# One normalisation and one transpose per slot, and the last 64 keys on GpSimd's queue, in a fused attention and MoE kernel

## The chip, the cores and the metric

The kernel runs on one core of a Trainium2 chip. A core has five engines that run side by side, each through its own instruction queue in order: TensorE (matmuls; PE, and PEld for its weight loads), VectorE (DVE), ScalarE (ACT), GpSimd (POOL) and SyncE (SP), which here only issues DMAs. DMAs are issued from a queue of an engine, run on 16 shared DMA engines, and tell by a semaphore when they have landed. The metric is the time of the device for one execution in microseconds (us). Before the change the median of 8 runs is 525.76 us (521.06 to 527.22).

## The reference

Thresholded attention, then a two-layer feed-forward block with a hard-swish gate. The shapes are 8 batches, 8 heads, 576 positions, head size 64; the block has 4608 rows, width 512 and inner width 2048.

```python
scores = scale * np.matmul(q, k.transpose(0, 1, 3, 2))
thresh = np.max(scores, axis=-1, keepdims=True) - tau
scores = np.where(scores >= thresh, scores, -1000000000.0)
attn = np.exp(scores - np.max(scores, axis=-1, keepdims=True))
attn = attn / (np.sum(attn, axis=-1, keepdims=True) + 1e-09)
x = np.matmul(attn, v)          # then heads side by side: [4608, 512]
h = x @ w_in
g = h * np.clip(h + 3.0, 0.0, 6.0) / 6.0
out = g @ w_out
```

## The kernel before

**Slots.** Four heads of one batch are a quad, two of them a pair; there are 16 quads. A quad is worked through in 9 slots: slots 0 to 3 take the first pair, 128 query rows each, slots 4 to 7 the second pair, and slot 8 the last 64 query rows of both pairs. That makes 144 slots, numbered n = 0 to 143. One loop over n writes all instructions of all engines in a hand-made order, and each engine runs its own in that order. A slot has two score tiles of 128 by 576, one per head.

**One slot's weights.** TensorE writes the scores into PSUM (`scores`, L287). VectorE copies them to the tile s in SBUF and takes the row maximum (`sm_max`, L302); GpSimd makes a bias from the maximum (L305). ScalarE masks by threshold (`sm_mask`, L309) and takes the exponential with the row sum (`sm_exp`, L314). VectorE inverts the sum (`sm_recip`, L317), GpSimd multiplies by it and writes bf16 into the tile pn (`sm_norm`, two instructions, L322). At the end of `sm_norm` SP issues a DMA that transposes pn into pT (or pR for slot 8), L330; in the first 21 slots TensorE does some of these transposes instead (`on_chip`). There are 4 buffers of pn and 4 of s. The product with the values (`multiply`, L346 and L349) comes some slots later, in columns of 256 queries.

**The loop from slot 22 on (N1 = 22).** In slot n VectorE takes the maxima for slot n + 1; ScalarE does the exponential of slot n and the mask of slot n + 1. Even slots start with the relu of the feed-forward block on ScalarE, odd ones do it on VectorE. In both, VectorE then does the gate (`mm1_gate`, L404), which reads the first matmul's PSUM bank (`mm1`, L381 or L376). After it in an even slot TensorE does two parts of the second matmul (`mm2_part`, L415), and then the next slot's `mm1` into the same bank. The product with the values and the scores of two later slots come in odd slots. Odd slots also finish the weights of two slots: the list `ready` holds the even slot and the odd one, whose reciprocals are taken in the odd slot (the even slot's after the maxima, L541; the odd slot's own near the end, L594), and both are normalised and transposed at its end (L613). The loop's end then issues waiting output DMAs (`flush`, L436), loads of q and k on SP (L620), and loads of values or of the block's weights on GpSimd (L622 to L625).

**Loads.** For quads 4 to 15, q and k come in blocks of 32 columns which VectorE transposes (`blocks_q`, L94, and `blocks_k`, L99, four DMAs each per pair of heads). The last 64 keys of each head go to the tile kr by two DMAs of 64 partitions (`rest`, L126), and TensorE transposes them (L257). `loads` is a list of jobs; a slot starts the next one, from slot 37 on only in even slots. The jobs of such a quad are: keys of the first pair, queries of the first pair, the last 64 keys with the keys of the second pair (`both`), queries of the second pair. Values come by GpSimd's queue (L143 and L146).

**After the loop.** The last products with the values are interleaved with the remaining feed-forward work: `av_main` for the last pair's first columns, the items left in `todo1`, eight items of the last batch, then the last columns and `av_rest`, which reads the transposed weights of slot 143.

Of the kernel before, what the change touches and what calls it, by code (L numbers as in the profile page):

```python
# [20 lines left out]
def kernel(  # L21
# [60 lines left out]
    def load_quad(quad):  # L82
        b, g = divmod(quad, 2)
        nat[quad] = (nat_pool.tile([P, 1152], F32, tag="nq", name="nq"),
                     nat_pool.tile([P, 4, 4, D], F32, tag="km", name="km"),
                     nat_pool.tile([P, 2 * D], F32, tag="kr", name="kr"))
        nq, km, kr = nat[quad]

        def main(dst, src, h, order, by=nc.sync):
            by.dma_start(out=dst[:, :, h, :], in_=src[b, 4 * g + h, 0:512, :].rearrange(order, t=4))  # L90

        def blocks_q(n, a, j):
            c = 32 * (2 * a + j)
            nc.sync.dma_start(out=nq[c:c + 32, n * S:(n + 1) * S].rearrange("p (k d) -> p k d", d=32),  # L94
                              in_=q[b, 4 * g + 2 * n + a, :, 32 * j:32 * j + 32].rearrange("(k r) d -> r k d", r=32))

        def blocks_k(n, a, j):
            c = 32 * (2 * a + j)
            nc.sync.dma_start(  # L99
                out=km[c:c + 32].rearrange("p t h d -> p (t h d)")[:, n * 512:(n + 1) * 512].rearrange(  # L100
                    "p (t m d) -> p t m d", t=4, d=32),
                in_=k[b, 4 * g + 2 * n + a, 0:512, 32 * j:32 * j + 32].rearrange("(m r t) d -> r t m d", r=32, t=4))

        def load_k(n):
            if b < NB:
                for a in range(2):
                    main(km, k, 2 * n + a, "(p t) d -> p t d")
            else:
                for a in range(2):
                    for j in range(2):  # L110
                        blocks_k(n, a, j)

        def load_q(n):
            if b < NB:
                for a in range(2):
                    main(nq[:, 0:1024].rearrange("p (t h d) -> p t h d", h=4, t=4), q, 2 * n + a, "(t p) d -> p t d",
                         by=nc.scalar if quad == n == 0 else nc.sync)
            else:
                for a in range(2):
                    for j in range(2):  # L120
                        blocks_q(n, a, j)

        def rest():
            for dst, src in ((kr[:], k), (nq[:, 1024:1152], q))[0:2 if b < NB else 1]:
                for n in range(2):
                    nc.sync.dma_start(out=dst[64 * n:64 * n + 64, :].rearrange("p (h d) -> p h d", h=2),  # L126
                                      in_=src[b, 4 * g + 2 * n:4 * g + 2 * n + 2, 512:S, :].rearrange("h p d -> p h d"))

        def both():
            rest()  # L130
            load_k(1)

        if b < NB:
            loads.extend((lambda: load_k(0), lambda: load_q(0), rest, lambda: load_k(1), lambda: load_q(1)))
        else:
            loads.extend((lambda: load_k(0), lambda: load_q(0), both, lambda: load_q(1)))

    def load_v(b):
        vm = v_pool.tile([P, H, 4 * D], BF16, tag="vm", name="vm")
# [176 lines left out]
    def sm_recip(sl):  # L316
        nc.vector.reciprocal(out=sl.rinv[:], in_=sl.rsum[:])  # L317

    def sm_norm(sl):
        sl.pn = pn = pn_pool.tile([P, 2, S], BF16, tag="pn", name="pn")  # L320
        for i in range(2):
            nc.gpsimd.tensor_scalar(out=pn[:, i, :], in0=sl.s[:, i, :], scalar1=sl.rinv[:, i:i + 1], scalar2=1.0,  # L322
                                    op0=Alu.mult, op1=Alu.mult)
        if sl.slot < 8:
            pair, t = 2 * sl.quad + sl.slot // 4, sl.slot % 4
            sl.dst = pts[pair][:, :, t * P:(t + 1) * P]
        else:
            sl.dst = ptr[sl.quad][:, :, :]
        if not sl.on_chip:
            nc.sync.dma_start_transpose(out=sl.dst, in_=pn[:].rearrange("p a b -> p (a b)"))  # L330
# [181 lines left out]
        return copies  # L512

    prev = None
    ready = []
    last_keys = []
    part = 0
    waiting = []
    for n, sl in enumerate(queue):
        quad, slot = sl.quad, sl.slot  # L520
        b, g = divmod(quad, 2)
        now = n
        if slot in (0, 4):
            pts[2 * quad + slot // 4] = pt_pool.tile([P, 9, 512], BF16, tag="pT", name="pT")
        if slot == 8:
            ptr[quad] = ptr_pool.tile([P, 9, P], BF16, tag="pR", name="pR")
        for ahead in {0: (1, 2), 9: (3,), 16: (4,)}.get(n, (quad + 2,) if quad > 2 and slot == (2 if quad == 3 else 0) else ()):
            if ahead < NQUAD:
                load_quad(ahead)
        if slot == 0 and g == 1 and b + 1 < B:  # L530
            load_v(b + 1)
        for copy in last_keys:
            copy()
        last_keys = []
        if 0 < n <= N1:
            for i in range(2):
                sm_exp(prev, i)
        if n + 1 < len(queue):
            sm_max(queue[n + 1])
        even = n >= N1 and n % 2 == 0  # L540
        for old in ready:  # L541
            sm_recip(old)
        for copy in waiting:
            copy()
        waiting = []

        if todo1:
            item, then = todo1.pop(0)
            h = mm1(item, OB if n > N1 and n % 2 and not pieces else HB)
            todo2.extend(then)  # L550
        else:
            item = None
        if n >= N1:
            for copy in multiply(n):
                copy()
        if item:
            mm1_gate(item, h, mm1_relu(h, on_act=even))
        copies = pe_transpose(queue[n - 2]) if n > 1 and queue[n - 2].on_chip else None
        if prev is not None and n < N1:
            sm_recip(prev)  # L560
        if copies:
            copies()
        pieces = 2 if n % 2 == 0 and todo2 else 0
        for _ in range(pieces):
            bb, mt, part = todo2.pop(0)
            mm2_part(bb, mt, part)
        if n <= N1:
            for i in range(2):
                sm_mask(sl, i)
        if n == N1:  # L570
            sm_recip(prev)
        if n >= N1:
            for i in range(2):
                sm_exp(sl, i)
            if n + 1 < len(queue):
                for i in range(2):
                    sm_mask(queue[n + 1], i)
        if n < N1:
            for copy in multiply(n):
                copy()  # L580
        if part == 3:
            waiting.append(lambda tile=(bb, mt): late.extend(mm2_out(*tile, on_act=False)))
            part = 0
        evict = []
        for job, of in turns.get(n, ()):
            if job == "k":
                (last_keys if even else evict).append(transpose_k(of))
            elif job == "q":
                if of // 2 not in qkT:
                    alloc_qk(of // 2)  # L590
                (waiting if even else evict).append(transpose_q(of))
            else:
                (last_keys if even else evict).append(transpose_rest(of, of_k=of > 0))
        if n >= N1 and not even:  # L594
            sm_recip(sl)
        for out_of_psum in evict:
            if out_of_psum:
                out_of_psum()
        if n == 0:
            warm_up(8)  # L600
        if n <= N1:
            scores(n + 2)
        elif n % 2:
            for m in (n + 3, n + 2):
                if m < len(queue):
                    scores(m)
        if n < 8:
            warm_up(6)
        if 0 < n <= N1:
            sm_norm(prev)  # L610
        if n >= N1:
            ready.append(sl)
        if n > N1 and not even:  # L613
            for old in ready:
                sm_norm(old)
            ready = []
        flush()
        if n == 0:
            start(loads, 2)
        elif n not in (4, 12, 15, 18, 21) and not 23 < n < 30 and (n < 37 or n % 2 == 0):  # L620
            start(loads, 1)
        if n < 4 or 15 < n < 20 or n > 33:  # L622
            start(vcasts, 1 if n < N1 or n % 2 else 0)
        else:
            start(casts, 2 if n in (5, 8, 11, 14) or 21 < n < 28 else 1)  # L625
        prev = sl
# [31 lines left out]
    av_main(2 * last + 1, 0, 256)()  # L658
    for item in todo1:
        rest1(*item, on_act=False)  # L660
    head, tail = moe_of(B - 1)
    for item in head:
        rest1(*item)
# [41 lines left out]
```

## Time and profile before

| | before |
|---|---|
| median of 8 runs | 525.76 us (521.06 to 527.22) |
| profiled execution, its time | 521.54 us |
| profiled execution, its span | 519.8 us |
| granted TensorE clock | 1.00 |
| TensorE busy | 506.1 us, 97% |
| VectorE, ScalarE, GpSimd busy | 441.7, 453.0, 285.4 us |
| DMAs issued by SP for q, k and kr blocks (L94, L99, L126) | 96, 96 and 40 |
| transposes issued by SP for pn | 131 |

The span runs from the first to the last instruction; the execution's own time has 1.7 us more around it. Times in the rows are us from the span's start. A row of a timeline gives start, length, engine, line, operation, output and input tiles, and in brackets the engine's idle time before it and what ended it. A row of the chain gives start, length and what the end of the program was waiting for then. "x4" at a row means that four instructions in succession are merged into it. SPq and POOLq are what the sequencers of SP and GpSimd do: they issue DMAs and wait. TensorE's busy share is high even where it is slowed, so lengths of whole slot pairs are compared where it matters.

### The profile page before, as it was taken

What the parts mean: (1) busy time and instruction counts of PE and PEld (TensorE: products, weight loads), DVE (VectorE), ACT (ScalarE), POOL (GpSimd) and SP (SyncE); (2) the same over time, 40 slices, a digit from 0 to 9 for tenths busy, and PEclk for the clock granted to TensorE, in tenths of its full rate; (3) what the DMA queues carried; (4) which work ended last, traced back from release to release, by engine and by line L of the source; (5) the groups of instructions that cost most, each with busy time, mean ns of one, the idle gap of its engine ahead of it and who ended that gap; (6) DMA issues with size and microseconds to landing.
All of it is one profiled execution on the core that took longest, in us unless ns stands there. A gap on an engine that the chain in (4) does not pass through costs nothing.

```text
span 519.8 us, 12073 instructions
## 1 busy us (share of the span) xinstructions
PE 506.1 (97%) x4145; PEld 321.3 (62%) x4145; DVE 441.7 (85%) x1124; ACT 453.0 (87%) x980; POOL 285.4 (55%) x514
## 2 busy tenths in 40 slices
PE   8999999999999999999999999999999999999997
PEld 6765556666665666666655666666655666668463
DVE  3788888999999999999999999999999999888151
ACT  4999979999999999999999999999999999995060
POOL 1788868855666665666556655666556655552000
PEclk9999999999999999999999999999999999999999
DMA  5899999979999898999999997999999996553222
GB/s 131 129 167 159 154 153 142 197 127 170 163 170 187 161 177 144 188 164 169 160 167 181 170 190 133 179 163 174 167 159 182 167 177 122 121 112 82 81 62 61
DMA packets 316780, 78.75 MB, mean 152 GB/s; under 512 B 299696, under 2 KB 312240, under 8 KB 316720
## 3 DMA queue, kind: packets, MB, share of 16 engines
q1 hardware_dynamic: 297920, 68.69, 75.1%
q0 software_dynamic: 17600, 8.92, 14.6%
q8 instruction: 32, 0.52, 0.4%
q10 hardware_dynamic: 1200, 0.39, 0.3%
q14 instruction: 28, 0.23, 0.2%
HBM read 36.70 MB, written 9.44 MB: 89 GB/s over the span
## 4 chain that ended last, share of the span: by engine, by line
PE 68%; ACT 8%; POOL 3%; DVE 3%; issue 2%; DMA 2%; SPq 0%; POOLq 0%; DVEq 0%
PE ps L415 20%; PE ps L287 20%; PE ps L381 18%; PE ps L346 6%; ACT s L309 4%; POOL pn L322 3%; ACT s L314 2%; PE ps L376 2%; ACT r L389 1%; PE ps L349 1%; DMA pT<-pn 1%; DVE s L302 1%; DVE g L404 1%; DMA g<-go 1%; ACT kT L222 0%
## 5 line engine op out<-in xcount | busy, mean ns | idle before, releaser
L322 POOL TENSOR_SCALAR pn<-s,rinv 128x576 bf16<-128x576 f32 x288 | 211.1, 745 | 82.5 <-issue 53.7
L302 DVE TENSOR_SCALAR_CACHE_REDUCE s<-ps 128x576 f32<-128x576 f32 x288 | 205.5, 751 | 15.2 <-PE ps L287 9.4
L309 ACT ACTIVATE s<-s,bias 128x576 f32<-128x576 f32 x288 | 205.9, 762 | 7.8 <-POOL bias L305 7.2
L314 ACT ACTIVATE s<-s 128x576 f32<-128x576 f32 x288 | 192.4, 670 | 0.3
L287 PE MATMUL ps<-kT,qT 64*128 64x384 f32 (+7 forms) x1280 | 174.0, 419 | 4.1 <-DVE s L302 3.1
L287 PEld LDWEIGHTS ps<-kT,qT 64*128 64x128 f32 (+1 forms) x1280 | 103.7, 175 | 58.6 <-issue 15.6
L415 PE MATMUL ps<-w_out_sb,g 128*128 128x512 bf16 x576 | 134.0, 379 | 0.0
L381 PE MATMUL ps<-xT,w_in_sb 128*128 128x256 bf16 x1024 | 130.8, 273 | 1.0 <-DVE g L404 0.7
L381 PEld LDWEIGHTS <-w_in_sb 128*128 128x128 bf16 x1024 | 95.4, 98 | 41.1 <-issue 21.7
L404 DVE SCALAR_TENSOR_TENSOR g<-r,ps 128x512 bf16<-128x512 f32 x128 | 87.5, 687 | 11.4 <-ACT r L389 7.4
L415 PEld LDWEIGHTS <-g 128*128 128x128 bf16 x576 | 56.2, 98 | 56.7
L305 POOL TENSOR_SCALAR bias<-m 128x2 f32<-128x2 f32 x144 | 27.2, 189 | 102.8 <-DVE rinv L317 84.2
L389 ACT ACTIVATE r<-ps,three 128x512 f32<-128x512 f32 x81 | 55.2, 687 | 26.8 <-PE ps L381 19.5
L314 ACT ACTIVATION_READ_ACCUMULATOR s<-s 128x1 f32 x288 | 54.3, 189 | 0.0
L391 DVE TENSOR_SCALAR r<-ps 128x512 f32<-128x512 f32 x63 | 42.9, 681 | 0.0
L346 PE MATMUL ps<-pT,vm 128*64 128x256 bf16 (+1 forms) x480 | 39.1, 285 | 0.0
L346 PEld LDWEIGHTS <-vm 128*64 128x64 bf16 x736 | 27.2, 110 | 16.0 <-issue 14.3
L357 DVE CAST xT<-ps 128x256 bf16<-128x256 f32 (+1 forms) x60 | 26.3, 438 | 12.6 <-PE ps L349 12.6
L423 DVE TENSOR_SCALAR osb<-ps 128x512 f32<-128x512 f32 x31 | 20.8, 673 | 12.6 <-PE ps L415 12.6
L302 DVE DVE_READ_ACCUMULATOR s<-ps 128x1 f32 x288 | 23.9, 83 | 0.0
L317 DVE RECIPROCAL rinv<-rsum 128x2 f32<-128x2 f32 x144 | 21.3, 148 | 2.6 <-ACT s L314 2.6
L143 POOL DMA_DIRECT2D vm<-in_v_dram x28 | 21.2, 758 | 0.1
(56 smaller groups left out, 244.1 us busy)
## 6 DMA issues: line engine op xcount, KB each, us to landing
out_dram<-osb SPq DMA_DIRECT2D x31, 256.0 KB, 2.6
nq<-in_q_dram SPq DMA_DIRECT2D x96, 72.0 KB, 3.4
km<-in_k_dram SPq DMA_DIRECT2D x96, 64.0 KB, 3.2
vm<-in_v_dram POOLq DMA_DIRECT2D x24, 128.0 KB, 4.1
km<-in_k_dram SPq DMA_DIRECT2D x16, 128.0 KB, 3.5
w_in_sb<-in_moe_w_in_dram POOLq DMA_DIRECT2D x16, 128.0 KB, 3.8
w_out_sb<-in_moe_w_out_dram POOLq DMA_DIRECT2D x16, 128.0 KB, 3.9
pT<-pn SPq DMA_TRANSPOSE x117, 3.7
```

What stands on the lines that cost most here:

```text
L287: nc.tensor.matmul(ps_flat[rows, c0:c0 + w], qT_of(pair)[a * 64:(a + 1) * 64, q0:q0 + rows.stop - rows.start], kT_of(pair)[a * 64:(a + 1) ...
L302: nc.vector.tensor_scalar(out=sl.s[:, i, :], in0=ps_flat[:, c0:c0 + S], scalar1=1.0, scalar2=None, op0=Alu.mult, op1=Alu.max, accum_out=sl ...
L305: nc.gpsimd.tensor_scalar(out=sl.bias[:], in0=sl.m[:], scalar1=-scale, scalar2=tau, op0=Alu.mult, op1=Alu.add)
L309: nc.scalar.activation(out=s, in_=s, func=Act.Prelu, bias=sl.bias[:, i:i + 1], scale=scale, alpha=REJECT)
L314: nc.scalar.activation(out=s, in_=s, func=Act.Exp, accum_out=sl.rsum[:, i:i + 1])
L322: nc.gpsimd.tensor_scalar(out=pn[:, i, :], in0=sl.s[:, i, :], scalar1=sl.rinv[:, i:i + 1], scalar2=1.0, op0=Alu.mult, op1=Alu.mult)
L346: nc.tensor.matmul(pb[a * 64:(a + 1) * 64, :], vm[:, 2 * hp + a, c * D:(c + 1) * D], pT[:, 5 * a + c, cols], start=(c == 0), stop=False)
L381: nc.tensor.matmul(ps[:, hb, n * 256:(n + 1) * 256], w_in_sb[:, ki, (ni + n) * P:(ni + n + 1) * P], xT[b][:, ki, c0:c0 + 256], start=(ki = ...
L389: nc.scalar.activation(out=r, in_=hps, func=Act.Relu, bias=three[:])
L391: nc.vector.tensor_scalar(out=r, in0=hps, scalar1=3.0, scalar2=0.0, op0=Alu.add, op1=Alu.max)
L404: nc.vector.scalar_tensor_tensor(out=out, in0=r, scalar=6.0, in1=hps, op0=Alu.min, op1=Alu.mult)
L415: nc.tensor.matmul(o_ps[0], gbuf[:, ni, mt * P:(mt + 1) * P], w_out_sb[:, ni, :], start=(ni == 0), stop=(ni == NI - 1))
```

## The change

From slot 22 on, each slot normalises the slot before it. An even slot's weights are thus treated where they were before, at the end of the following odd slot; an odd slot's reciprocal moves to the following even slot, after that slot's maxima, and its normalisation and transpose move to that slot's end. The list `ready` is gone. The last slot's are placed after the loop, behind the items of `todo1`. For quads 4 to 15 the two loads of the last 64 keys go out from GpSimd's queue instead of SP's, and the load jobs have another order: queries, keys, queries of the second pair, then the last 64 keys with the second pair's keys.

```diff
-                    nc.sync.dma_start(out=dst[64 * n:64 * n + 64, :].rearrange("p (h d) -> p h d", h=2),
+                    (nc.sync if b < NB else nc.gpsimd).dma_start(out=dst[64 * n:64 * n + 64, :].rearrange("p (h d) -> p h d", h=2),
                                       in_=src[b, 4 * g + 2 * n:4 * g + 2 * n + 2, 512:S, :].rearrange("h p d -> p h d"))
...
-            loads.extend((lambda: load_k(0), lambda: load_q(0), both, lambda: load_q(1)))
+            loads.extend((lambda: load_q(0), lambda: load_k(0), lambda: load_q(1), both))
...
-    ready = []
...
-        for old in ready:
-            sm_recip(old)
+        if n > N1:
+            sm_recip(prev)
...
-        if n >= N1 and not even:
-            sm_recip(sl)
...
-        if 0 < n <= N1:
+        if n > 0:
             sm_norm(prev)
-        if n >= N1:
-            ready.append(sl)
-        if n > N1 and not even:
-            for old in ready:
-                sm_norm(old)
-            ready = []
...
     for item in todo1:
         rest1(*item, on_act=False)
+    sm_recip(prev)
+    sm_norm(prev)
     head, tail = moe_of(B - 1)
```

## The prediction

> **What bounds the kernel now.** I read the busy shares first, then the chain that ended last in an undisturbed stretch, then the places where that chain leaves TensorE, then the queue that they lead to.
>
> ```profile
> PE 506.1 (97%) x4145; PEld 321.3 (62%) x4145; DVE 441.7 (85%) x1124; ACT 453.0 (87%) x980; POOL 285.4 (55%) x514
> PE 68%; ACT 8%; POOL 3%; DVE 3%; issue 2%; DMA 2%; SPq 0%; POOLq 0%; DVEq 0%
> ```
>
> Four engines are above 84%, so a share alone settles nothing. The chain between 254 and 282 us does (start, length, work):
>
> ```profile
> 261.09 2.14 PE ps L287 x16
> 263.23 0.98 PE ps L381 x8
> 264.21 1.73 PE ps L415 x8
> 265.93 0.87 PE ps L381 x8
> 266.81 0.56 PE ps L346 x8
> 267.37 0.11 PE ps L349 x2
> 267.47 2.14 PE ps L287 x16
> ```
>
> One even and one odd slot take 6.39 us, all of it TensorE. Nearly every pair from 105 to 462 us repeats this, so no work taken from another engine shortens a pair. What can change is only how often TensorE is made to wait. Inside a pair one wait is close: the second matmul group of L381 reuses the bank that the first filled, so it follows ScalarE's relu and VectorE's gate. The timelines of the three engines (start, length):
>
> ```profile
> 264.25 0.69 ACT L389 ACTIVATE r<-ps,three 128x512 f32<-128x512 f32 x1 [0.31 <-PE ps L381]
> 264.96 0.69 DVE L404 SCALAR_TENSOR_TENSOR g<-r,ps 128x512 bf16<-128x512 f32 x1
> 265.77 1.04 PE L381 MATMUL ps<-xT,w_in_sb 128*128 128x256 bf16 x8
> ```
>
> The gate ends at 265.65 and TensorE goes on at 265.77; where TensorE really waited it went on 0.05 us after the gate. So this ring has about 0.07 us to spare per pair, and anything that makes the relu or the gate later is paid.
>
> Three pairs from 105 us on are too long for what they hold. By the starts of the score matmuls: 331.98 to 338.77 is 6.79 us against 6.50 for a pair of the same make-up (273.77 to 280.27); 338.77 to 345.68 is 6.91 against 6.72 (280.27 to 286.99); 397.15 to 404.45 is 7.30 against 6.72. That is 0.29 + 0.19 + 0.58 = 1.06 us. The chain of the first two, in parts, leads back to a transpose:
>
> ```profile
> 322.47 5.13 DMA pT<-pn
> ...
> 331.47 0.19 POOL bias L305
> ...
> 331.69 1.44 ACT s L309 x2
> ...
> 342.99 0.70 DVE g L404
> ...
> 343.73 1.03 PE ps L381 x8
> ```
>
> GpSimd could not overwrite the pn buffer of four slots before, as its transpose had not landed; bias, mask, relu and gate then came late. Why the transpose was late, SP's queue shows:
>
> ```profile
> 314.21 2.71 SPq L330 DMA_TRANSPOSE pT<-pn  x2
> 317.01 1.20 SPq L436 DMA_DIRECT2D out_dram<-osb  x2
> 318.25 1.40 SPq L126 DMA_DIRECT2D kr<-in_k_dram  x2
> 319.70 2.66 SPq L99 DMA_DIRECT2D km<-in_k_dram  x4
> 322.47 2.87 SPq L330 DMA_TRANSPOSE pT<-pn  x2
> ```
>
> These rows fill 10.8 of 11.1 us. The weights of slot 94 were ready at 314.14 and SP issued their transpose only at 322.47. Adding SP's issue times from 105 to 424 us in stretches of 29 us gives 25.7 to 27.8 us in each: SP is almost as full as TensorE.
>
> The third place is GpSimd's own order: the bias for the odd slot stands behind the odd slot's normalisation and a load.
>
> ```profile
> 393.34 1.46 POOL L322 TENSOR_SCALAR pn<-s,rinv 128x576 bf16<-128x576 f32 x2 [1.22 <-issue]
> 395.40 0.67 POOL L146 DMA_DIRECT2D vr<-in_v_dram  x1 [0.60 <-issue]
> 396.15 0.19 POOL L305 TENSOR_SCALAR bias<-m 128x2 f32<-128x2 f32 x1
> ```
>
> **The change, part by part.** Even slots keep their place: they are still normalised at the end of the next, odd slot. What moves is the odd slot's normalisation, from its own end to the end of the next even slot.
>
> *VectorE.* The reciprocal passes the two maxima of the even slot and now stands just ahead of the gate. At 263.42 it held the first maximum up by 0.04 us; in odd slots, after the maxima, the next instruction starts 0.08 us after it. Net +0.04 us ahead of the gate, inside the 0.07 us: I take 0. The upper end is its whole recorded 0.16 us with no gain before: 0.16 - 0.07 = 0.09 us in each of 57 pairs, 5.1 us. A gain below 0 is possible too: it no longer makes the maxima wait where ScalarE's exp is late. It adds no wait, since ScalarE does the exp before the relu that the gate needs anyway.
>
> *GpSimd.* The two multiplies (1.47 us) pass the values loads and the bias of the next slot but one. That bias can start when its maximum is there, at about 394.7 instead of 396.15: the 0.58 us goes. Behind the moved multiplies stand the next bias and the even slot's multiplies, which are then due about 2 us later.
>
> *The last 64 keys.* Two loads per quad leave SP for GpSimd, 24 in all for quads 4 to 15. The near row is the values load L146, of the same 64-partition form, 0.65 us each: 1.3 us of GpSimd per quad, after the odd slot's multiplies. They end at about 268.0 in the pair above, when the next bias can start at 267.1; its mask starts at 268.83, so 0.6 us of cover stays, and I take 0. Without that cover the price is 0.9 us per quad, 11 us. The Trainium skill ("DMA: Bandwidth & Descriptors", SWDGE vs HWDGE vs iDMA) speaks against this: GpSimd writes its descriptors to SBUF, where VectorE's two-port modes can lock it out. Here 16 such loads took 645 to 672 ns beside a VectorE that is over 90% busy, so the row decides: 0.65 us, no stall.
>
> On SP 1.3 us per quad of about 29 us goes. The same page (Issuing engines are not separate DMA queues) says that spreading issues over engines saves only sequencer time, usually small beside the transfer. By the rule this part is worth 0. By the rows SP's time is what the transposes wait for, so with the new order it is worth the other 0.48 us.
>
> *SP's order.* One transpose stands at the end of each slot, instead of two in odd ones. The odd slot's passes an output, and up to slot 36 a load; the loads of the even slot now stand behind it. For a pair I get 2 x 1.35 transposes + 2.7 loads + 0.55 output = 5.95 of 6.39 us, where a pair with the 64 keys had 7.3: the delay should fall from 8 us to under 3, and a buffer is needed again only 11.3 us after its multiplies end. Each weight is used 4 or more slots later, so the odd transpose, 1.5 us later, costs nothing.
>
> *Load order.* q, k, q, then the keys' rest and k: each is still issued 6 or more slots ahead of its transpose; 0.
>
> *Slots 22 to 30.* ScalarE bounds 76 to 98 us. It waits for a late bias 0.17 us at 91.76 and 0.03 at 98.18: -0.2 us. The two key loads of slot 22 fall among weight loads; 0, as above.
>
> *The tail.* The last slot's reciprocal moves behind two gates, from 470.46 to 473.44; its multiplies end at 475.21 and the transpose, 3.2 us to landing like the last six, at 478.4. TensorE reads it at 478.66: 0. With the 4.3 us that transposes to this buffer take at the median it is 0.9 us.
>
> Sum: 521.54 - 0.48 - 0.58 - 0.2 = 520.28 us for the profiled execution.
>
> **From this execution to the median.** The runs shown have a median 4.22 us above it and spread over 6 us. TensorE's own work doesn't vary, so I read part of this as more stalls of the kind above. If all were, the median would fall to 520.3; if none, to 525.76 - 1.26 = 524.5. I take the middle: **522.4 us**, its own range 520.3 to 524.5.
>
> **Rivals.**
> 1. *Only the visible stalls go*, and the excess is something else: 524.5, or 525.8 if the transposes stay late. For it: TensorE is 97% busy, and the stalls reach it in three pairs of 57. Against: such a spread is not that of TensorE's work.
> 2. *The gate ring becomes the bound.* The reciprocal ahead of the gate costs more than 0.07 us. In some 17 pairs the second maximum ends no earlier than the relu, so there is no idle VectorE time to hide it. At 0.09 us net in each of 57 pairs: 524.5 + 5.1 = 529.6. It is slower by 0.5% once the gate is 0.14 us later: 57 x 0.07 = 4.0 less 1.26.
> 3. *The key loads on GpSimd make the bias late*: 12 x 0.9 = 11 us at worst if the 0.6 us of cover is gone in every quad, more likely in a few.
>
> **How the numbers follow.** 0.5% (2.6 us) is about what a measurement of this kernel can tell from no change. Gain beyond that, below 523.1: 0.52. Only the visible part or nothing, 523.1 to 528.4: 0.27. Rivals 2 and 3 above 528.4: 0.21. The range from 519.5 to 529.0 takes in the full excess at one end and most of rival 2 at the other.
>
> **What would show it.** Transposes issued within 3 us of the multiplies; no wait of GpSimd's multiplies for a transpose; the bias 0.3 to 1.4 us earlier in even slots; all pairs at 6.39 to 6.72 us. I am wrong if TensorE waits for the gate in most pairs, if the mask waits for the bias after key loads, or if TensorE waits at the last values product.

## The result and the profile after

| | before | after |
|---|---|---|
| median | 525.23 us (521.01 to 528.19, 53 runs) | 522.01 us (521.47 to 523.32, 18 runs) |
| ratio of the times, 95% interval | | 0.995 [0.993, 0.997] |
| profiled execution, time and span | 521.54 and 519.8 us | 521.73 and 520.0 us |

The kernel is 0.5% faster, and the median lies 0.4 us from the forecast. But the two profiled executions are equally long. The gain is in the other executions of before, which reach up to 528 us and no longer do after the change. The page of after shows the same bound: TensorE's share is unchanged, and GpSimd has the 24 added loads.

```profile
PE 505.8 (97%) x4145; PEld 321.3 (62%) x4145; DVE 442.5 (85%) x1124; ACT 451.9 (87%) x980; POOL 299.3 (58%) x538
PE 78%; ACT 3%; DVE 2%; DMA 1%; issue 1%; POOL 0%; POOLq 0%; DVEq 0%
```

In the second row, the shares of the chain that ended last, TensorE rises from 68% to 78% and ScalarE falls from 8% to 3%. The three long pairs are now 6.50, 6.79 and 6.71 us (before 6.79, 6.91 and 7.30), and the pair at 91.85 us is 0.18 us shorter. The last pair starts at 454.70 us, 1.14 us earlier than before.

SP's queue in the stretch around 314 us (start, length, work, "x4" for four issues in succession):

```profile
313.99 1.18 SPq L436 DMA_DIRECT2D out_dram<-osb  x2
315.26 1.33 SPq L330 DMA_TRANSPOSE pT<-pn  x1
316.63 2.22 SPq L94 DMA_DIRECT2D nq<-in_q_dram  x4
318.97 2.83 SPq L330 DMA_TRANSPOSE pT<-pn  x2
321.86 2.71 SPq L99 DMA_DIRECT2D km<-in_k_dram  x4
324.67 1.90 SPq L330 DMA_TRANSPOSE pT<-pn  x1
```

The two key loads are gone from it. Over 105 to 424 us (319 us) SP's issues add up to 283.1 us instead of 294.8, and SP's gaps of over 0.15 us add up to 14.9 us instead of 2.5. So before the change SP's queue was hardly ever idle.

The 1.14 us were lost again behind the last pair. The chain of after in the tail:

```profile
472.61 0.74 POOL pn L322
473.35 0.73 POOLq L693
474.10 4.32 DMA pR<-pn
478.42 0.04 issue
478.46 0.32 PE ps L346 x8
```

TensorE had nothing else to do and stood still for 0.80 us until the last slot's weights had landed. The second matmul starts at 478.90 us, only 0.17 us earlier than before, so 0.97 us of the 1.14 is gone there. A later wait of TensorE, for the gate of the last rows, grew from 0.21 to 0.57 us. That makes the span 0.2 us longer than before.

**A measure for what follows.** For the slots 37 to 129 two quantities can be read from the rows. *The wait for SP* is the time from the end of a slot's multiplies to the start of its transpose's issue on SP. *The slack* is the time from the landing of the transpose to the first product with the values that reads it. At a slack of 0.04 us TensorE, or its weight load, goes on as soon as the weights are there. Even slots have the smallest slack: half of them are read five slots later, and as their multiplies run at the end of the slot after, only four slots remain. The table gives both for one profiled execution of each kernel, with the times. In after, e3, e4 and e11 the trace lacks 9 to 16 of the 131 landings, and the smallest slack there is that of the others. Single executions differ: after and e4 have the same loop, and yet the even slots wait 2.53 us in the one and 4.02 in the other. A difference of 1.5 us in this column can be such a spread. Four chips were used, and the kernel before is not equally fast on them: its medians are 526.34, 522.84, 524.31 and 524.94 us for e1 to e4, e5 to e8, e9 to e11 and e12. Each ratio is against before on the same chip; that of e1 leaves out one slow execution (536.54 us).

| kernel | median us (range) | ratio, 95% interval | wait for SP, median even / odd | smallest slack | TensorE waits for pT |
|---|---|---|---|---|---|
| before | above | 1 | 5.15 / 4.67 | 0.11 | 0 |
| after | above | 0.995 [0.993, 0.997] | 2.53 / 0.26 | 1.06 | 0 |
| e1 per-slot order alone | 530.35 (528.55 to 536.54) | 1.0086 [1.0057, 1.0115] | 6.67 / 4.07 | 0.04 | 7.2 |
| e2 key queue alone | 521.33 (521.12 to 522.01) | 0.9909 [0.9877, 0.9941] | 3.38 / 2.35 | 0.82 | 0 |
| e3 fifth pn buffer | 526.75 (521.93 to 529.06) | 1.0007 [0.998, 1.0034] | 5.47 / 4.75 | 0.04 | 3.0 |
| e4 after, tail earlier | 521.75 (520.81 to 524.63) | 0.9916 [0.9891, 0.9941] | 4.02 / 1.99 | 0.04 | 0.4 |
| e5 per-slot order, loads first | 524.81 (521.31 to 528.11) | 1.0031 [1.001, 1.0052] | 4.99 / 5.38 | 0.04 | 2.0 |
| e6 e2 and two spare loads on SP | 525.16 (521.9 to 528.02) | 1.0019 [0.9998, 1.004] | 4.87 / 4.17 | 0.04 | 0.3 |
| e7 before, a longer execution | 523.09 (one run) | | 4.71 / 3.73 | 0.04 | 0.3 |
| e8 load order alone | 523.05 (521.59 to 528.38) | 0.9994 [0.9971, 1.0016] | 5.06 / 4.03 | 0.04 | 0 |
| e9 outputs on GpSimd | 525.71 (525.28 to 526.47) | 1.0025 [1.0005, 1.0045] | 3.53 / 2.89 | 0.13 | 0 |
| e10 after, keys back on SP | 527.29 (525.54 to 530.71) | 1.0068 [1.0046, 1.009] | 6.01 / 3.65 | 0.04 | 3.9 |
| e11 keys and outputs on GpSimd | 526.24 (525.69 to 526.92) | 1.0033 [1.0013, 1.0052] | 1.72 / 0.89 | 1.24 | 0 |
| e12 as e6, spare loads on GpSimd | 521.57 (521.12 to 522.26) | 0.994 [0.9919, 0.9961] | 2.36 / 1.56 | 1.12 | 0 |

### The profile page after: what moved, and what is told of

The parts are those of the page before. It is cut to its first block, busy times and chain, and to the rows that moved or that the text cites. A ratio compares the mean times of both kernels' runs of the same rounds, so it can differ in the third digit from the quotient of the medians.

```text
span 520.0 us, 12124 instructions
## 1 busy us (share of the span) xinstructions
PE 505.8 (97%) x4145; PEld 321.3 (62%) x4145; DVE 442.5 (85%) x1124; ACT 451.9 (87%) x980; POOL 299.3 (58%) x538
## 4 chain that ended last, share of the span: by engine, by line
PE 78%; ACT 3%; DVE 2%; DMA 1%; issue 1%; POOL 0%; POOLq 0%; DVEq 0%
PE ps L287 24%; PE ps L415 24%; PE ps L381 19%; PE ps L346 6%; PE ps L376 2%; ACT s L309 1%; PE ps L349 1%; ACT s L314 1%; DMA pR<-pn 1%; ACT r L389 1%; DMA g<-go 1%; DVE s L302 1%; DVE g L404 1%; POOL pn L322 0%; PE ps L257 0%
## 5 line engine op out<-in xcount | busy, mean ns | idle before, releaser
L381 PE MATMUL ps<-xT,w_in_sb 128*128 128x256 bf16 x1024 | 130.8, 273 | 1.2 <-DVE g L404 0.7
L381 PEld LDWEIGHTS <-w_in_sb 128*128 128x128 bf16 x1024 | 95.5, 98 | 41.0 <-issue 22.0
L346 PE MATMUL ps<-pT,vm 128*64 128x256 bf16 (+1 forms) x480 | 39.1, 285 | 0.0
L346 PEld LDWEIGHTS <-vm 128*64 128x64 bf16 x736 | 27.2, 110 | 16.9 <-issue 15.5
L317 DVE RECIPROCAL rinv<-rsum 128x2 f32<-128x2 f32 x144 | 23.0, 160 | 0.6 <-ACT s L314 0.6
```

The lines of the kernel that those rows point to most:

```text
L346: nc.tensor.matmul(pb[a * 64:(a + 1) * 64, :], vm[:, 2 * hp + a, c * D:(c + 1) * D], pT[:, 5 * a + c, cols], start=(c == 0), stop=False)
L381: nc.tensor.matmul(ps[:, hb, n * 256:(n + 1) * 256], w_in_sb[:, ki, (ni + n) * P:(ni + n + 1) * P], xT[b][:, ki, c0:c0 + 256], start=(ki = ...
```

## The experiments

**The parts of the change, each alone.** e1 is the kernel before with the per-slot order and nothing else.

```diff
-        for old in ready:
-            sm_recip(old)
+        if n > N1:
+            sm_recip(prev)
...
-        if n >= N1 and not even:
-            sm_recip(sl)
...
-        if 0 < n <= N1:
+        if n > 0:
             sm_norm(prev)
...
-        if n > N1 and not even:
-            for old in ready:
-                sm_norm(old)
-            ready = []
...
+    sm_recip(prev)
+    sm_norm(prev)
```

> One transpose per slot from slot 22 on, but the last 64 keys stay on SP and the load order stays as before. My theory (a full SP queue delays transposes, and GpSimd's old order makes the bias late; each gives a part): 523.0 to 524.2 us, with transposes as late as before and some waits of GpSimd for a pn buffer left. If the order on GpSimd and VectorE is all of the gain: 522.0 to 522.6. If SP's queue is all of it: 524.8 to 525.8.

Measured: slower, 1.0086 [1.0057, 1.0115]; 530.35 us is above all three ranges of the expectation. The waits of TensorE between 76 and 480 us (what waited, for what: us in total, times, the longest), and the chain at one of the seven waits in the first row, of 1.36 us:

```profile
PE ps L346 <- DMA pT<-pn: 7.2, 7, 1.7
PE ps L287 <- DVE s L302: 2.2, 3, 1.0
PE ps L381 <- DVE g L404: 0.7, 1, 0.7
```

```profile
180.55 1.33 DVE s L302 x3
181.88 3.45 DMA pT<-pn
185.33 0.04 issue
185.37 0.63 PE ps L346 x8
```

The first row is new, and with 7.2 us it is nearly the whole difference of the two profiled spans (527.4 against 519.8 us). It is a wait that the prediction had ruled out: TensorE at the product with the values, for weights not yet transposed. The third row, the wait for the gate, is what it was before. So the ring of relu and gate is not what costs here.

e2 is the kernel before with only the queue of the last 64 keys changed for quads 4 to 15.

```diff
-                    nc.sync.dma_start(out=dst[64 * n:64 * n + 64, :]...
+                    (nc.sync if b < NB else nc.gpsimd).dma_start(out=dst[64 * n:64 * n + 64, :]...
```

> Only the last 64 keys of quads 4 to 15 go out from GpSimd's queue; odd and even slots are still finished together and the load order is as before. My theory: 523.5 to 524.8 us, since the transposes come earlier but the bias of odd slots still stands behind the odd slot's multiplies. If SP's queue is all of the gain: 522.0 to 522.6. If the order is all of it: 525 or, through 1.3 us more on GpSimd per quad ahead of a bias, up to 527.

Measured: 0.9909 [0.9877, 0.9941], and all executions within 0.9 us. At 521.33 us it is better than the expectation's theory; the alternative that SP's queue is all of the gain came closest. The same view has no row with pT any more:

```profile
PE ps L287 <- DVE s L302: 1.5, 2, 1.1
PE ps L381 <- DVE g L404: 0.7, 1, 0.7
```

On the same chip the whole change with an earlier tail (e4) reaches 0.9916 [0.9891, 0.9941], so this one edit gives as much as the whole change. e8 is the load order alone.

```diff
-            loads.extend((lambda: load_k(0), lambda: load_q(0), both, lambda: load_q(1)))
+            loads.extend((lambda: load_q(0), lambda: load_k(0), lambda: load_q(1), both))
```

> The kernel before with the new order of the load jobs alone (queries, keys, queries, the last 64 keys with the second keys; all on SP). Every load is still 6 or more slots ahead: 525 to 527 us, no change. If the order matters to the transposes behind it: up to 2 us either way.

Measured: 0.9994 [0.9971, 1.0016], nothing. e10 is the changed kernel with the keys' queue put back.

```diff
-                    (nc.sync if b < NB else nc.gpsimd).dma_start(out=dst[64 * n:64 * n + 64, :]...
+                    nc.sync.dma_start(out=dst[64 * n:64 * n + 64, :]...
```

> The changed kernel with nothing undone but the queue of the last 64 keys, which SP issues again: the per-slot order and the load order together. Theory (the order costs, the key queue gains, the load order is nothing): 1.004 to 1.011, like the per-slot order alone (1.0086), with TensorE waiting for pT at the values product. Rival (the load order is what makes the per-slot order work): 0.996 to 1.002.

Measured: 1.0068 [1.0046, 1.009], with this row among TensorE's waits:

```profile
PE ps L346 <- DMA pT<-pn: 3.9, 6, 1.2
```

The theory holds: with the keys on SP the new order costs 0.7 to 0.9%, with either load order.

**Which wait costs the time: the pn buffer or the product?** The prediction traced the late transposes to GpSimd, which waits for a pn buffer, and then to a late gate. e3 gives the kernel before a fifth pn buffer, and pays for it with one buffer less of kr.

```diff
+    kr_pool = ctx.enter_context(tc.tile_pool(name="krp", bufs=2))
...
-    pn_pool = ctx.enter_context(tc.tile_pool(name="pn", bufs=4))
+    pn_pool = ctx.enter_context(tc.tile_pool(name="pn", bufs=5))
...
-                     nat_pool.tile([P, 2 * D], F32, tag="kr", name="kr"))
+                     kr_pool.tile([P, 2 * D], F32, tag="kr", name="kr"))
```

> The kernel before with 5 buffers of pn instead of 4 (and 2 of kr instead of 3, to make room): a transpose may be 3.2 us later before GpSimd has to wait for it. If the wait for a pn buffer is what costs the time in executions above 522: 522 to 523, with no wait of GpSimd's multiplies for a transpose. If the bias behind the odd slot's multiplies is what costs it: 525, no change.

Measured: 1.0007 [0.998, 1.0034]. GpSimd's wait for a transpose (3.7 us, three times, in before) is gone, and the two pairs that the prediction traced to it are as short as it said: 6.50 and 6.72 us instead of 6.79 and 6.91. But the time is not shorter. In the profiled execution two other pairs lost 4.1 us, 3.0 of them in this wait of TensorE (L347 is L346 of the other kernels):

```profile
PE ps L347 <- DMA pT<-pn: 3.0, 1, 3.0
```

TensorE waited another 0.9 us for a gate, which had itself waited for the transpose of the feed-forward block's tile go. SP issues that transpose too.

e7 is the kernel before, unchanged, for the profile of an execution longer than the first one.

> The kernel before once more, for a profile of one of its longer executions. My theory now: above 523 us TensorE waits for pT at the values product for about the difference to 521.5. If the excess is elsewhere (start of the kernel, outputs at the end): no such waits and the same pairs of slots as in the first profile.

Its span is 521.3 us, 1.5 us longer. Most of that is not what the theory expected: 1.04 us are lost before the first scores, in TensorE's first matmuls. The rows of the first execution, then of this one (start, length):

```profile
5.01 0.60 PE L232 MATMUL ps<-identf,km 128*128 128x128 f32 x4
5.45 0.60 PE L185 MATMUL ps<-identf 128*128 128x128 f32 x4
```

```profile
5.08 1.09 PE L232 MATMUL ps<-identf,km 128*128 128x128 f32 x4
5.96 1.06 PE L185 MATMUL ps<-identf 128*128 128x128 f32 x4
```

The same instructions took nearly twice as long there, and the first scores started at 7.89 us instead of 6.85. Other kernels start late as well (8.10 us in e4 and e11, 7.71 in e6). So this part belongs to the execution and not to the kernel. The wait that the theory named is there too, but it is the smaller part. The chain between 300 and 310 us:

```profile
302.25 0.50 SPq L94
302.74 0.05 issue
302.79 0.02 SPq L330
302.81 0.04 issue
302.85 4.26 DMA pT<-pn
307.11 0.04 issue
307.15 0.63 PE ps L346 x8
```

SP issues four loads of queries, then the transpose. This lands 4.26 us later, and TensorE, done with L381 at 306.84, has waited for it. It is slot 88, which in the first profiled execution had 0.11 us of slack. This pair takes 6.77 us instead of 6.39, which is 0.38 of the 1.5 us. So the kernel before stands on an edge: some 0.1 us more on SP and TensorE stops.

No longer execution of before than this one was profiled, so what fills them is not shown. The runs hold one more sign of it: the granted clock. Of the 176 executions of before that ran beside the experiments, 67 have a mean granted clock of 0.997 or less, and all of these take 525.26 us or more (median 526.49). The other 109 have a median of 522.66 us, and five of them are above 525.26. At 0.997 the missing clock is at most 0.003 x 525 = 1.6 us, an estimate, so it is not the whole difference. After the key loads have left SP no execution shows it (after 0 of 18, e2 0 of 7, e4 0 of 11, e12 0 of 22). Whether the clock falls because TensorE has stood still, or for another reason, is not shown: in e10's profiled execution TensorE waits 3.9 us for pT, and all 22 executions are at 0.998 or more.

**Why the new order costs: do the loads stand behind a waiting transpose?** In e1 the odd slot's transpose stands at the end of the even slot, ahead of that slot's loads. The idea is that SP reaches it before its multiplies are done and holds the loads up, and that the next even slot's transpose stands behind them. e5 is e1 with the loads issued ahead of the transpose from slot 24 on.

```diff
+        if n > 23:
+            if not 23 < n < 30 and (n < 37 or n % 2 == 0):
+                start(loads, 1)
         if n > 0:
             sm_norm(prev)
...
-        elif n not in (4, 12, 15, 18, 21) and not 23 < n < 30 and (n < 37 or n % 2 == 0):
+        elif n < 24 and n not in (4, 12, 15, 18, 21):
             start(loads, 1)
```

> The single-transpose kernel (keys on SP, old load order) with each slot's loads issued ahead of its transpose instead of behind it, from slot 24 on. If that kernel's 4 us are the cost of loads that stand behind the odd slot's transpose, which waits for its multiplies: 525 to 527 us. If they come from something else in the order (the transpose of an even slot still waits behind everything in a full queue): 529 to 532.

Measured: 1.0031 [1.001, 1.0052] against 1.0086 for e1, and 2.0 us of waits:

```profile
PE ps L346 <- DMA pT<-pn: 2.0, 3, 1.1
```

The even slots wait 4.99 us for SP instead of 6.67, the odd ones 5.38 instead of 4.07. So the place of the loads in SP's queue makes up most of e1's loss: 0.31% is left of 0.86%. The two ran on different chips, and their intervals lie only 0.05% apart. How the place acts is not shown. That SP is held up by a waiting transpose is not what e1's trace shows where TensorE waits. From slot 32 to slot 128 SP stood idle ahead of an odd slot's transpose only once, for 0.44 us, and its gaps of over 0.15 us between 105 and 424 us add up to 1.4 us, less than before's 2.5. SP was busy and further behind: at the even slots with a slack of 0.04 us in e1, the wait for SP is 1.2 to 2.7 us longer than in before. What put it there stays open. In e1's profile the key loads took longer each (0.69 us instead of 0.65), but so did e2's (0.69), without a loss.

**Is it SP's time, or the bytes?** e6 is e2 with two more loads per quad on SP. They read the last 64 keys a second time into a tile that nothing reads.

```diff
         def both():
             rest()
+            spare = spare_pool.tile([P, 2 * D], F32, tag="spare", name="spare")
+            for n in range(2):
+                nc.sync.dma_start(out=spare[64 * n:64 * n + 64, :]...
             load_k(1)
```

> The keys-on-GpSimd kernel with two more loads per quad put on SP in the place of the moved ones: they read the same 64 keys into a spare tile that nothing reads. If SP's issue time is what the kernel before lacks: back to 525 to 527.5 us, with TensorE waiting for pT at the values product. If it is the queue on which the keys travel, or what stands behind them: 521 to 522.5, as without the loads.

Measured: 525.16 us, 1.0019 [0.9998, 1.004]. The gain is gone, and the executions spread over 6 us again. But e6 also moves more bytes, so e12 moves the same bytes and issues the two spare loads from GpSimd:

```diff
-                nc.sync.dma_start(out=spare[64 * n:64 * n + 64, :]...
+                nc.gpsimd.dma_start(out=spare[64 * n:64 * n + 64, :]...
```

> The kernel of the doubled key loads once more, but the two extra loads per quad, which are never read, go out from GpSimd too: GpSimd issues four 64-partition loads per quad, SP none, and the DMA engines move the same extra bytes. Theory (the queue that issues them is what costs): TensorE does not wait for pT, all executions lie close together like with the keys alone, 521.0 to 522.5 us, on a chip whose kernel before has a median of 523 to 526; GpSimd's 1.3 us more per quad stay covered. Rival (it was the extra bytes on the DMA engines that brought the time back): 524 to 526 us with executions spread over 5 us or more. Second rival (GpSimd full, the bias late as with the outputs there): above 523.5 us, executions close together, with waits of TensorE for the gate.

Measured: 521.57 us (521.12 to 522.26), ratio 0.994 [0.9919, 0.9961]. The theory holds and both rivals fall: the extra bytes cost nothing that can be measured, and GpSimd has room for four such loads per quad. What cost the time is the queue that issues them. e6 and e12 ran on two chips, but their intervals, each against before on its own chip, do not meet.

**Does any work taken from SP help?** e9 takes the outputs from SP instead of the keys, e11 both.

```diff
     def flush():
         for o, i in late:
-            nc.sync.dma_start(out=i, in_=o)
+            nc.gpsimd.dma_start(out=i, in_=o)
```

> The kernel before with nothing changed but the queue of the output DMAs (L436), which GpSimd issues instead of SP. Theory (SP's issue time is what the late transposes cost; any work taken from SP helps): about 4 outputs of 0.6 us leave SP per two quads, roughly the same per quad as the two key loads, so a ratio of 0.990 to 0.996 and no wait of TensorE for pT at the values product. Rival (it is the key loads themselves that matter, their place or their DMA queue): 0.998 to 1.002. Second rival (GpSimd has no room: an output stands ahead of the next bias): above 1.002, with the mask waiting for the bias.

> The kernel before with the last 64 keys and the outputs both on GpSimd's queue. Theory: after the keys alone (0.9909) SP no longer makes TensorE wait, so taking the outputs too adds nothing: 0.989 to 0.993. Rival (part of the stalls is still SP's): 0.984 to 0.988. Rival (GpSimd gets too full): above 0.995, with the mask waiting for the bias.

Measured: 1.0025 [1.0005, 1.0045] and 1.0033 [1.0013, 1.0052], where the theory expected 0.990 to 0.996 and 0.989 to 0.993. Part of it came true: TensorE's wait for pT is gone, and all executions of each lie within 1.3 us. But other waits took its place. In e9's waits:

```profile
ACT s L309 <- POOL bias L305: 8.9, 18, 1.1
PE ps L381 <- DVE g L404: 3.0, 6, 0.8
```

In before these are 1.6 us, 3 times, and 0.7 us, once. GpSimd's timeline in e9, and TensorE's 6 us later (in brackets the idle time before and what ended it):

```profile
194.95 1.17 POOL L436 DMA_DIRECT2D out_dram<-osb  x2
196.11 0.74 POOL L143 DMA_DIRECT2D vm<-in_v_dram  x1
196.94 0.46 POOL L305 TENSOR_SCALAR bias<-m 128x2 f32<-128x2 f32 x2
```

```profile
203.30 1.03 PE L381 MATMUL ps<-xT,w_in_sb 128*128 128x256 bf16 x8 [0.82 <-DVE g L404]
```

Two outputs of 0.6 us stand, with a values load, between the multiplies and the bias. Then the mask, relu and gate are late, and TensorE waits. This pair takes 7.88 us instead of 6.71. It is the mechanism of rival 3, a late bias, with the outputs as its cause. The key loads escape it by their place. GpSimd's timeline of e2 at the same slots:

```profile
194.90 0.18 POOL L305 TENSOR_SCALAR bias<-m 128x2 f32<-128x2 f32 x1
195.14 1.28 POOL L126 DMA_DIRECT2D kr<-in_k_dram  x2
196.49 0.19 POOL L305 TENSOR_SCALAR bias<-m 128x2 f32<-128x2 f32 x1
```

They stand between two biases: the one that the next mask needs is done, and the other has time. In e9 both biases stand behind the outputs. No run moves the outputs to a better place in GpSimd's order, so the place as the cause is read from these rows.

**The tail.** e4 is the changed kernel with the last slot's reciprocal, multiplies and transpose ahead of the last columns' product and the items of `todo1`.

```diff
+    sm_recip(prev)
+    sm_norm(prev)
     av_main(2 * last + 1, 0, 256)()
     for item in todo1:
         rest1(*item, on_act=False)
-    sm_recip(prev)
-    sm_norm(prev)
```

> The kernel after, with the last slot's reciprocal and multiplies placed right after the loop, ahead of the left-over feed-forward items. The profile after has TensorE wait 0.80 us for the last transpose at 478.46; that goes: 521.1 to 521.4 us, with pR's transpose issued about 2.9 us earlier. If the wait only moves to the next one in the tail (the transpose of go): 522.0, no change.

Measured: 0.9916 [0.9891, 0.9941], 521.75 us. In its trace TensorE reads the last weights without a wait, so the 0.80 us are gone there. But the median is not below that of e2 on the same chip (521.33 us), so what e4 saves in the tail does not show against e2. Its expectation of 521.1 to 521.4 us was missed. Its profiled execution also has a wait for pT in the middle (0.4 us), in the loop where after has none, so the changed kernel is not wholly free of them.

## Why the prediction was right, and where it was not

**The sum for the profiled execution** was 520.28 us and it took 521.73. The visible stalls and slots 22 to 30 were to give 1.26 us; 1.14 us had been gained at the last pair. The failing term is the tail. "0" was taken there, for a landing of 3.2 us, and 0.9 us named as the other end, for 4.3. The transpose took 4.32 us and TensorE waited 0.80. The longer wait for the last gate (0.36 us) was in no step.

**From this execution to the median** half of an excess of 4.22 us was to go. Practically all of it went: the median of after is 0.28 us above its profiled execution, where that of before is 3.69 us above its own (525.23 - 521.54). The two errors, 1.45 us too little in the sum and 1.83 us too much in the excess, nearly cancel. That the forecast lies as close as 0.4 us to the median is therefore luck. The premise of this step, "TensorE's own work doesn't vary", was wrong as well: e7 lost 1.04 us in TensorE's own first matmuls, and before's executions above 525.26 us come nearly all with a lower granted clock. Taking the middle of two bounds was a guess, and what the excess was made of stays open in part.

**SP's full queue as the cause** was right for the gain, and e6 against e12 shows it. The weighing of the rule was right too: the Trainium skill's "DMA: Bandwidth & Descriptors" (Issuing engines are not separate DMA queues) lets only sequencer time be saved by another issuing engine. That sequencer time was worth 0.9% in e2 and 0.6% in e12, since the weights wait behind it.

**How SP's delay reaches TensorE** was wrong. The prediction followed the path of the profiled execution, by the pn buffer and a late bias. That path was right for its 0.48 us in that execution, and e3 shortened the same two pairs by as much. But the median did not move (e3). The step that failed is "Each weight is used 4 or more slots later, so the odd transpose, 1.5 us later, costs nothing". For slot 88 of before, four slots are 10.66 us from the end of the multiplies to the product, and its transpose landed after 10.54 us; the median landing is at 8.68 us. The odd slot's transpose does have the time (a slack of 4.65 us or more in after); the even slot's, which waited 6.67 us for SP in e1 instead of 5.15, does not. Why the new order makes it wait longer stays open. In e1 and e10 TensorE waited 7.2 and 3.9 us for such transposes, where the prediction had put 0.

**The share of the parts** was wrong for the same reason. The per-slot order was to bring 0.58 us through the bias, and 0.48 was to come from SP together with the key loads. In e1 no mask waits for a bias from 105 us on (in before 1.6 us, 3 times), so that gain was real, yet the kernel is 0.9% slower. In the runs the order is harmless only with the keys off SP: e4, order and queue, is at 0.9916, and e2, the queue alone, at 0.9909.

**SP's delay of under 3 us** holds for 68 of the 93 slots from 37 to 129 (median 1.78 us, at most 6.13), and in e4, with the same loop, for 45 (median 3.08 us). Its sum took 1.35 us for a transpose's issue. That is near the median in before (1.37); the mean, which a sum needs, is 1.53 us, and the 5.95 us become 6.3 of 6.39. **The reciprocal ahead of the gate** cost 0, as taken: TensorE's wait for the gate is 0.7 us, once, in before and after alike, so rival 2 did not come. **The key loads on GpSimd** took 0.63 us each for the 0.65 taken, without a late bias, so rival 3 did not come from them; e9 shows that its mechanism is real when the load stands at another place. **The load order** is 0, as taken. **The busy shares**: three engines are above 84%, not four, which changes nothing in the argument.

## What to carry to other kernels

A queue that is nearly full does not show in the busy shares. Add up its issue times over a steady stretch, and then look for the smallest slack between a transfer's landing and its reader over all repetitions, not in one that looks typical. Where the smallest slack is near zero, a move that adds to that queue or changes its order can cost more than it seems. Before a DMA is moved to a computing engine's queue, look at what stands right behind it there: the same 0.6 us was free in one place (e2) and cost more than it gained in another (e9).

One profiled execution is not enough for this: before's first one was among its fastest, and its stalls were not those that cost e1, e3 and e10 their time.

The fastest kernels here are e2 (521.33 us) and e12 (521.57 us): the kernel before with the one queue changed. Whether e2 is faster than the changed kernel was not measured on one chip; e4, which differs from that only in the tail, has an interval that overlaps e2's.

## What the runs showed of the hardware

The sum of SP's issue times is not the same in every execution. In e2, 14.5 us of key loads left SP between 105 and 424 us, and the sum of SP's issues fell by 4.9 us only (294.8 to 289.9); in e9, 16.0 us of outputs left and the sum rose to 297.0 us. But after and e4, with the same loop, have 283.1 and 292.2 us, so what moved the sum in e2 and e9 cannot be told from one execution of each.

The same matmuls can take different times at the start of an execution: four of L232 took 0.60 us in one profiled execution of before and 1.09 in another, and the first scores start 6.85 to 8.10 us after the first instruction in the kernels here. A difference of 1 us between two profiled executions can lie there.

The spread of the executions differs between kernels. On all four chips before ranges over 7 us or more. e2, e9, e11 and e12 have all their executions within 1.3 us, whether they are faster or slower; after has 1.9 us. It is not the key loads' queue alone: e4, without them on SP, has 3.8 us (520.81 to 524.63).
